# One batch's k and q loads cast to fp16 by their DMA, and the last unit's outputs stored by whole token blocks

## The chip, the cores and the metric

The kernel runs on one core of a Trainium2 chip. The metric is the device time of one execution in microseconds (us). Engines are named as in the profile: PE is TensorE's matrix products and PEld its weight loads, DVE is VectorE, ACT is ScalarE, POOL is GpSimd, SP is SyncE. SP, ACT and POOL also issue DMAs; in a view, SPq, ACTq and POOLq are those issues.

## The reference

Two steps. Linear attention over q, k, v of shape (8 batches, 8 heads, 576 tokens, 64), and a sum of four dense experts over the 4608 tokens of width 512:

```python
q_p, k_p = (phi(q), phi(k))               # phi(x) = (x if x > 0 else exp(x) - 1) + 1
kv = np.einsum('bhsd,bhse->bhde', k_p, v)
z = np.sum(k_p, axis=2)
num = np.einsum('bhsd,bhde->bhse', q_p, kv)
den = np.einsum('bhsd,bhd->bhs', q_p, z)[..., None] + 1e-06
x = num / den                             # then (batch, token, head * 64) as rows of 512
...
p = domain_probs / (domain_probs.sum(-1, keepdims=True) + 1e-09)
for e in range(E):                        # E = 4, w1 512 x 1024, w2 1024 x 512
    h = np.maximum(x @ w1[e], 0.0)
    out += p[:, e:e + 1] * (h @ w2[e])
```

## The kernel before, in words

**Tiles.** A batch's first 512 tokens make one tile of the expert part; the 64 left over of all eight batches make a ninth. So there are nine tiles, `j` = 0 to 8, and with four experts 36 units `(j, e)`. Inside a unit the first product (`Block`, L719 to L782) and the second (`layer2_product`, L643) each use a scheme with seven half-size products in place of eight; GpSimd and VectorE form the sums of operands that it needs (`hidden_sum` L628, `token_sum` L695, `weight_sums` L601, `weight_sums2` L615). Only expert 0 of tile 0, and the second products of tile 0, run in the plain form (`layer1_group` L520, `layer2_part` L574).

**The order of the work.** The program is written out by hand: the lists in `CFG` give each step a position, the steps are sorted by it (L995), and every engine executes its own steps in that order. An instruction that waits holds up everything behind it on its engine. Batch 0's attention comes first (`START`), filled up with warm-up products (L860). Batch `j + 1`'s attention is interleaved with the expert units of tile `j`.

**The loads of the start.** Batch 0 is loaded by SP and ACT. All weights and batch 1's inputs go through GpSimd's queue in the order of `CFG["DMA"]` (`load_first`, L188): first-layer and second-layer weights `w<layer><expert><half>`, cast from fp32 to fp16 by the DMA itself, and batch 1's parts between them: `k0` to `k3`, `q0` to `q3`, `v0` to `v3`, each two heads by 512 tokens, 256 KB in fp32, and `lk`, `lv` for the leftover tokens. In the list's later half: `w110, w111, k0, w120, w121, v0, w210, lk0, w211, lv1, k1, k2, lv0, v1, w131, w130, v2, k3, v3, q1, q0, w220, w221, q2, q3, w230, w231`. The four `v` parts are given fp16 homes (`hs1`, `hs3`), so their DMA casts. Seven of the eight k and q parts have no home of their own: they take fp32 buffers of the pool `praw` (tag `raw`, six buffers, tile name `rawb`). `q2` takes an accumulator's buffer (`acc`, tile name `rawu`). From batch 2 on the inputs are loaded by SP in fp32, into the same `raw` buffers.

**Who reads the parts.** For batch 1, `phi_act` (L303) runs two ScalarE instructions on each k or q part: L310 writes x + 1 as fp16 into `kp` or `qp`, L315 writes exp(x) into PSUM (`psum_ee`). `phi_dve` (L318) then combines the two on VectorE at L322, and does not read the raw part. A v part is copied by ScalarE at L332. `weight_sums` for an expert needs that expert's first-layer weights (L605 is its first instruction).

**The end.** `add_acc` (L562) adds each second product, scaled by the token's probability, to the block's fp32 accumulator (`acc`, 128 tokens x 512 columns). For the last unit, `(8, 3)`, the products come in the order 1, 2, 6, 5, 7, 3, 4, each for the blocks i = 0 and 1 (`layer2_product`, with p the product's number), and alternate between two PSUM banks. Products 1 and 2 end columns 0 to 255 of block i, product 3 ends its columns 256 to 511; product 7 ends columns 256 to 511 of block 2 + i, and product 4 its columns 0 to 255. `store` (L548) writes to the output. A block of tile 8 holds the 64 leftover tokens of two batches, so it takes two DMAs: SP stores the upper half of the partitions, ACT the lower. In the last unit each column half is stored when its last product is added, which makes 16 DMAs of 64 x 256 (64 KB).

Of the kernel before, what the change touches and what calls it, by code (L numbers as in the profile page):

```python
# [10 lines left out]
FP32 = mybir.dt.float32  # L11
FP16 = mybir.dt.float16
# [68 lines left out]
def kernel(  # L81
# [10 lines left out]
    nc = tc.nc  # L92
    ATTN, HSUM, L2ORD, L2AT, MODE = (CFG[x] for x in ("ATTN", "HSUM", "L2ORD", "L2AT", "MODE"))

    B, H, S, D = q.shape
    N, E = moe_domain_probs.shape
    _, Dm, F = moe_w1.shape
# [4 lines left out]
    SM = CM * P  # L102
# [7 lines left out]
    NTILES = N // NT  # L110
# [46 lines left out]
    praw = ctx.enter_context(tc.tile_pool(name="praw", bufs=NRAW))  # L157
# [15 lines left out]
    out_b = out.rearrange("(b s) d -> b s d", s=S)  # L173
# [64 lines left out]
    class Batch:  # L238
# [21 lines left out]
        def load(self, name, i, eng=nc.sync, home=None):  # L260

            src = {"q": q, "k": k, "v": v}[name]
            shape = [P, HQ, CM, D]
            if home is None:
                t = praw.tile(shape, FP32, tag="raw", name="rawb")
            elif home == "h":
                if i % 2 == 0:
                    self.pairs[name] = pm.tile([P, HG, CM, D], FP32, tag="h", bufs=NHB, name="rawh")
                t = self.pairs[name][:, i % 2 * HQ : (i % 2 + 1) * HQ]
            elif home[:2] == "hs":  # L270
                t = pm.tile(shape, FP16, tag=home, bufs=2, name="rawv")
            else:
                t = pm.tile(shape, FP32, tag=home, bufs={"u2": 2, "u3": 1, "acc": NACC}[home], name="rawu")
            h0 = i * HQ
            eng.dma_start(
                out=t, in_=src[self.b, h0 : h0 + HQ, 0:SM].rearrange("h (p c) d -> p h c d", c=CM)
            )
            self.raw[name, i] = t
# [236 lines left out]
    accs = {}  # L515
# [29 lines left out]
    def new_py():  # L545
        return ppm.tile([P, Dm], FP32, tag="py", bufs=2, name="py")

    def store(j, ns, cols=slice(0, Dm)):  # L548
        acc = accs[j, ns][:, cols]
        if j < B:  # L550
            nc.sync.dma_start(
                out=out_b[j, 0:SM].rearrange("(p c) d -> c p d", c=CM)[ns],
                in_=acc,
            )
        else:
            for u in range(2):
                (nc.scalar if u else nc.sync).dma_start(
                    out=out_b[2 * ns + u, SM:S, cols],
                    in_=acc[u * HP : (u + 1) * HP],
                )  # L560

    def add_acc(j, e, ns, ps, ds, first):  # L562
        if (j, ns) not in accs:
            accs[j, ns] = pm.tile([P, Dm], FP32, tag="acc", bufs=NACC, name="acc")
        acc = accs[j, ns][:, ds]
        pscal = p_sb[:, j, ns, e : e + 1]
        if first:
            nc.scalar.activation(acc, ps, AF.Identity, scale=pscal)  # L568
        else:
            nc.vector.scalar_tensor_tensor(  # L570
                out=acc, in0=ps, scalar=pscal, in1=acc, op0=AO.mult, op1=AO.add
            )

    def layer2_part(j, e, ns, hT, part, parts):  # L574
        if part == 0:
            pys[ns] = new_py()
        py = pys[ns]
        for fj in range(part * FC // parts, (part + 1) * FC // parts):
            nc.tensor.matmul(  # L579
                out=py,  # L580
                lhsT=rows(hT, fj)[:, ns * P : (ns + 1) * P],
                rhs=w2_sb[e][:, fj, :],
                start=(fj == 0),
                stop=(fj == FC - 1),
            )
        if part == parts - 1:
            add_acc(j, e, ns, py, slice(0, Dm), e == 0)
            if e == E - 1:
                store(j, ns)
# [53 lines left out]
    def layer2_product(j, e, hT, hss, p, i):  # L643


        if (j, e) == (NTILES - 1, E - 1):
            if p == 1:
                pys[i] = [ppm.tile([P, DH], FP32, tag=tag, bufs=2, name=f"p{tag}") for tag in ("b", "e")]
            run, side = pys[i]
        else:  # L650
            if p == 2:
                pys[i] = new_py()
            run, side = pys[i][:, 0:DH], pys[i][:, DH:Dm]
        ts = slice(i * P, (i + 1) * P)
        ts2 = slice(NH + i * P, NH + (i + 1) * P)
        w, tw = w2_sb[e], t2_sb[e]
        lo, hi = slice(0, FH), slice(FH, FC)
        ps, lhsT, rhs, first = {
            1: (run, lambda k: hT[k // 2][:, k % 2, 0, ts], w[:, lo, 0:DH], (j, e) == (NTILES - 1, E - 1)),
            2: (side, lambda k: hT[k // 2][:, k % 2, 1, ts], w[:, hi, 0:DH], True),  # L660
            5: (side, lambda k: hss[k // 2][0][:, k % 2, ts], tw[:, 0], True),
            6: (run, lambda k: hss[k // 2][1][:, k % 2, ts], tw[:, 1], False),
            7: (run, lambda k: hT[k // 2][:, k % 2, 0, ts2], w[:, lo, DH:Dm], False),
            3: (side, lambda k: hss[k // 2][3][:, k % 2, ts], w[:, hi, DH:Dm], False),
            4: (run, lambda k: hT[k // 2][:, k % 2, 1, ts2], tw[:, 2], False),
        }[p]
        for k in range(FH):
            nc.tensor.matmul(  # L668
                out=ps,
                lhsT=lhsT(k),  # L670
                rhs=rhs[:, k],
                start=first and k == 0,
                stop=k == FH - 1,
                skip_group_check=True,
            )
        c1, c2 = slice(0, DH), slice(DH, Dm)
        ns, ds, first = {
            2: (i, c1, True),
            5: (2 + i, c2, True),
            1: (i, c1, False),  # L680
            6: (i, c2, True),
            7: (2 + i, c2, False),
            3: (i, c2, False),
            4: (2 + i, c1, True),
        }[p]
        add_acc(j, e, ns, ps, ds, first and e == 0)
        if (j, e) == (NTILES - 1, E - 1):
            if p in (2, 3, 4, 7):
                store(j, ns, ds)
        elif e == E - 1 and p in (3, 4):  # L690
            store(j, ns)

    tts = {}

# [107 lines left out]
    def batch_steps(bt, nxt, put, at, at_next):  # L802
# [21 lines left out]
        for m, (n, i) in enumerate(mine):  # L824
            if n == "v":
                put(at[n][i], bt.vcast, i)
            else:
                put(at[n][i], bt.phi_act, n, i)
                put(at[n + "d"][i], bt.phi_dve, n, i)
            if not first:  # L830
                put(at[n][i] + 1, load, m + NRAW)
# [9 lines left out]
        if first:  # L841
            put(at["qtl"], bt.pe_qTl)
            put(at["xl"], bt.pe_xl)
            for i in range(NPAIR):
                put(at["qt"][i], bt.pe_qT, i, nc.scalar)
                put(at["nd"][i], bt.nd_pair, i)
                put(at["xt"][i], bt.pe_xT, i)
            for i in range(NRAW):
                put(at["next"][i], load, len(mine) + i)
        else:  # L850
            put(at["qT"], bt.dma_qT)
            for i in range(6):
                put(at["nd"][i], numerators, 3 * i, min(3, NPAIR * CM - 3 * i))
# [12 lines left out]
    with tc.manual_schedule(  # L866
# [87 lines left out]
        for n, (j, e) in enumerate(units):  # L954
            h, hss = [None, None], [[None] * 4, [None] * 4]
            at = base + 2 * NSLOT * n
            for d in range(2):
                put_block(at + d * NSLOT, j, e, d, h)
            at += 2 * NSLOT + LAG

            def hsum(d, i, hT=h, hss=hss):
                hidden_sum(hT[d], hss[d], i)

            for d in range(2):
                for i in range(4):
                    put_at(at + HSUM[d][i], hsum, d, i)
            order = L2ORD
            if n == len(units) - 1:
                order, at = (1, 2, 6, 5, 7, 3, 4), at + NSLOT
            for m in range(14):  # L970
                put_at(at + L2AT[m], layer2_product, j, e, h, hss, order[m // 2], m % 2)
# [56 lines left out]
```

## Time and profile before

| | us |
|---|---|
| median of 4 runs | 496.43 (495.97 to 496.99) |
| profiled execution, its own time | 496.37 |
| its span (first to last instruction) | 494.5 |
| PE busy in the span | 482.3 |
| last matmul's row begins / last accumulator add ends | 488.55 / 490.11 |
| last store issue begins (SP / ACT) | 491.08 / 491.39 |

Read it so. The span is what the engines' records cover; the execution's own time is 1.87 us longer. The page has busy time by engine, a row of digits over 40 slices of 12.36 us, the chain that ended last (followed back from the last instruction to what released each step), the costliest groups of instructions, and the DMA issues with the time to landing. The trace answers further questions: the waits of one engine in a stretch of time, busy times by stretch, and a list in order of time.

For the loads of the start, these are the landings on GpSimd's queue, each worked out as the start of the issue plus its time to landing (us): w111 30.75, k0 31.4, w120 33.8, w121 36.2, v0 37.0, w210 39.6, lk0 39.7, w211 42.3, lv1 42.5, k1 43.5, k2 44.2, lv0 44.5, v1 44.85, w131 47.3, w130 49.85, v2 50.5, k3 51.2, v3 51.9, q1 52.5, q0 53.25, w220 56.2, w221 60.2, q2 61.2, q3 62.2, w230 64.6. They are read by ScalarE at: k0 31.39, k1 49.69, k2 51.73, k3 53.29, q0 and q1 57.43 and 59.57, q2 61.57, q3 63.56.

### The profile page before, as it was taken

To read this page: it belongs to the slowest core of one execution; us is meant where nothing else is said; L and a number is where in the kernel's file an instruction comes from. 1 tells how busy PE (TensorE), PEld (TensorE's weight loads), DVE (VectorE), ACT (ScalarE), POOL (GpSimd) and SP (SyncE) were. 2 spreads that over 40 slices of the span, in tenths; PEclk is the share of its full clock that TensorE was granted. 3 is DMA by queue.
4 is the path that set the end of the run, shared out by engine and by line. 5 is a ranking of instruction groups with operands and counts; after the bars stand their busy time and mean duration, and the time that the engine had idled before them with its cause. 6 is when DMAs were issued, how large, how long until landed. Compare 5 with 4: busy or idle time off the path is not lost.

```text
span 494.5 us, 11616 instructions
## 1 busy us (share of the span) xinstructions
PE 482.3 (98%) x4346; PEld 409.3 (83%) x4346; DVE 379.1 (77%) x802; ACT 336.4 (68%) x678; POOL 354.5 (72%) x339
## 2 busy tenths in 40 slices
PE   7999989999999999999999999999999999999995
PEld 3556656888898989898989898989898888888884
DVE  5757988798867987698859886888687756775686
ACT  5766969964978488848894789468954565446530
POOL 3735204778967797769776977698669877987774
PEclk9999999999999999999999999999999999999998
DMA  8999976542454245533464245523231020002003
GB/s 257 206 219 238 273 145 177 165 111 52 110 188 116 55 111 162 131 69 93 134 166 80 71 150 139 102 59 91 84 77 32 5 95 1 1 2 86 1 1 87
DMA packets 82201, 53.66 MB, mean 109 GB/s; under 512 B 46240, under 2 KB 75936, under 8 KB 82144
## 3 DMA queue, kind: packets, MB, share of 16 engines
q1 hardware_dynamic: 70592, 40.07, 31.1%
q0 software_dynamic: 9824, 11.27, 12.2%
q10 hardware_dynamic: 1728, 1.57, 1.2%
q8 instruction: 34, 0.56, 0.5%
q14 instruction: 23, 0.19, 0.1%
HBM read 45.16 MB, written 9.44 MB: 110 GB/s over the span
## 4 chain that ended last, share of the span: by engine, by line
PE 83%; DMA 5%; DVE 4%; ACT 4%; POOL 2%; issue 1%; SPq 0%; POOLq 0%; DVEq 0%; ACTq 0%
PE py L668 37%; PE pb L733 23%; PE pe L733 17%; DMA w<-in_moe_w_dram 3%; PE py L579 3%; DVE acc L570 1%; PE psum_nd L465 1%; DMA rawb<-in_v_dram 1%; PE psum_kv L425 1%; DMA out_dram<-acc 1%; ACT u L744 1%; ACT psum_ee L315 1%; POOL w L183 1%; DMA rawh<-in_q_dram 1%; DVE h L717 1%
## 5 line engine op out<-in xcount | busy, mean ns | idle before, releaser
L570 DVE SCALAR_TENSOR_TENSOR acc<-py,p_sb,acc 128x256 f32<-128x256 f32 (+1 forms) x382 | 182.5, 489 | 49.2 <-PE py L668 40.0
L717 DVE CUSTOM_DVE_ANT_0 h<-pe,u 128x512 f16<-128x512 f32 x140 | 96.4, 688 | 41.7 <-PE pe L733 25.4
L733 PEld LDWEIGHTS <-w 128*128 128x128 f16 x1120 | 108.9, 98 | 17.0 <-issue 1.8
L635 POOL TENSOR_TENSOR hs<-h 128x512 f16<-128x512 f16 x64 | 73.9, 1155 | 55.0 <-DVE h L717 53.6
L668 PEld LDWEIGHTS <-h 128*128 128x128 f16 x1024 | 99.6, 98 | 12.2 <-issue 0.9
L668 PE MATMUL py<-w,h 128*128 128x256 f16 x744 | 106.4, 273 | 0.2 <-ACT acc L568 0.2
L744 ACT COPY u<-pb 128x512 f32<-128x512 f32 x140 | 82.8, 592 | 27.5 <-PE pb L733 25.1
L637 POOL TENSOR_TENSOR hs<-hs,h 128x512 f16<-128x512 f16 x64 | 74.7, 1167 | 27.1 <-PE py L668 24.5
L733 PEld LDWEIGHTS <-s 128*128 128x128 f16 x840 | 81.6, 98 | 11.8 <-DVE s L607 0.7
L733 PE MATMUL pb<-tt,w 128*128 128x256 f16 x560 | 84.0, 272 | 0.8 <-ACT u L744 0.7
L668 PEld LDWEIGHTS <-hs 128*128 128x128 f16 x768 | 74.4, 98 | 9.9 <-issue 1.3
L641 POOL TENSOR_TENSOR hs<-h,hs 128x512 f16<-128x512 f16 x64 | 74.5, 1165 | 3.6 <-PE py L668 2.9
L668 PE MATMUL py<-t,hs 128*128 128x256 f16 x496 | 74.4, 272 | 0.6 <-DVE acc L570 0.4
L639 POOL TENSOR_TENSOR h<-h 128x512 f16<-128x512 f16 x64 | 74.5, 1163 | 0.0
L759 ACT ACTIVATE h<-pe 128x512 f16<-128x512 f32 x70 | 41.8, 598 | 44.9 <-PE pe L733 44.4
L753 ACT COPY pe<-pb 128x512 f32<-128x512 f32 x70 | 40.2, 575 | 41.5 <-PE pb L733 14.9
L777 ACT ACTIVATE h<-pb 128x512 f16<-128x512 f32 x70 | 41.9, 599 | 10.4 <-PE pb L733 10.3
L733 PE MATMUL pb<-tt,s 128*128 128x256 f16 x280 | 42.0, 273 | 0.4 <-DVE s L607 0.4
L733 PE MATMUL pe<-tt,s 128*128 128x256 f16 x280 | 42.0, 273 | 0.0
L733 PE MATMUL pb<-xT,w 128*128 128x256 f16 x248 | 37.2, 273 | 0.1
L733 PE MATMUL pe<-xT,s 128*128 128x256 f16 x248 | 37.2, 273 | 0.0
L668 PE MATMUL py<-w,hs 128*128 128x256 f16 x248 | 37.2, 273 | 0.0
(120 smaller groups left out, 604.4 us busy)
## 6 DMA issues: line engine op xcount, KB each, us to landing
out_dram<-acc SPq DMA_DIRECT2D x32, 256.0 KB, 2.5
w<-in_moe_w_dram POOLq DMA_DIRECT2D x14, 512.0 KB, 12.7
rawb<-in_v_dram SPq DMA_DIRECT2D x26, 256.0 KB, 2.8
rawb<-in_q_dram SPq DMA_DIRECT2D x26, 256.0 KB, 2.9
rawb<-in_k_dram SPq DMA_DIRECT2D x26, 256.0 KB, 3.3
w<-in_moe_w_dram POOLq DMA_DIRECT2D x4, 256.0 KB, 6.4
rawb<-in_k_dram POOLq DMA_DIRECT2D x4, 256.0 KB, 10.8
rl<-in_q_dram SPq DMA_DIRECT2D x16, 64.0 KB, 2.6
```

What stands on the lines that cost most here:

```text
L570: nc.vector.scalar_tensor_tensor(out=acc, in0=ps, scalar=pscal, in1=acc, op0=AO.mult, op1=AO.add)
L635: nc.gpsimd.tensor_tensor(out=hs[0], in0=a21, in1=a22, op=AO.add)
L637: nc.gpsimd.tensor_tensor(out=hs[1], in0=hs[0], in1=a11, op=AO.subtract)
L639: nc.gpsimd.tensor_tensor(out=a21, in0=a11, in1=a21, op=AO.subtract)
L641: nc.gpsimd.tensor_tensor(out=hs[3], in0=a12, in1=hs[1], op=AO.subtract)
L668: nc.tensor.matmul(out=ps, lhsT=lhsT(k), rhs=rhs[:, k], start=first and k == 0, stop=k == FH - 1, skip_group_check=True,)
L717: nc.vector._custom_dve(TENSOR_ADD_SAT, out=out, in0=ps, in1=u, s0=BIG, s1=0.0)
L733: nc.tensor.matmul(out=ps[:, kk], lhsT=lk(kc), rhs=rhs[:, kc], start=first and kk == 0 and kc == 0, stop=kc == 1, skip_group_check=True,)
L744: nc.scalar.copy(u, self.b)
L753: nc.scalar.copy(self.e5, self.b)
L759: nc.scalar.activation(self.h[:, :, 0, 0:NH], self.e5, AF.Relu)
L777: nc.scalar.activation(self.h[:, :, 1, 0:NH], self.b, AF.Relu)
```

## The change

Two edits. In `load`, a part without a home is an fp16 tile if it is batch 1's and its name is k or q; the DMA, which GpSimd issues, then casts as it does for v. That holds for k0 to k3, q0, q1 and q3; q2 has the home `acc` and stays fp32, and the leftover parts (`rl`) stay fp32. The buffers of tag `raw` stay six. In `store`, the columns are no longer chosen: the last unit stores a whole block of 128 x 512 after product 3 (blocks 0 and 1) and after product 4 (blocks 2 and 3), again with one DMA by SP and one by ACT, so eight DMAs of 64 x 512 (128 KB). Nothing is stored after products 2 and 7.

Apart from these stores, each engine has the same instructions in the same order with the same waits.

```diff
@@ -262,7 +262,8 @@
             src = {"q": q, "k": k, "v": v}[name]
             shape = [P, HQ, CM, D]
             if home is None:
-                t = praw.tile(shape, FP32, tag="raw", name="rawb")
+                cast = self.b == 1 and name in "kq"
+                t = praw.tile(shape, FP16 if cast else FP32, tag="raw", name="rawb")
             elif home == "h":
                 if i % 2 == 0:
                     self.pairs[name] = pm.tile([P, HG, CM, D], FP32, tag="h", bufs=NHB, name="rawh")
@@ -545,8 +546,8 @@
     def new_py():
         return ppm.tile([P, Dm], FP32, tag="py", bufs=2, name="py")
 
-    def store(j, ns, cols=slice(0, Dm)):
-        acc = accs[j, ns][:, cols]
+    def store(j, ns, last=False):
+        acc = accs[j, ns]
         if j < B:
             nc.sync.dma_start(
                 out=out_b[j, 0:SM].rearrange("(p c) d -> c p d", c=CM)[ns],
@@ -554,8 +555,8 @@
             )
         else:
             for u in range(2):
-                (nc.scalar if u else nc.sync).dma_start(
-                    out=out_b[2 * ns + u, SM:S, cols],
+                (nc.scalar if last and u else nc.sync).dma_start(
+                    out=out_b[2 * ns + u, SM:S],
                     in_=acc[u * HP : (u + 1) * HP],
                 )
 
@@ -684,11 +685,8 @@
             4: (2 + i, c1, True),
         }[p]
         add_acc(j, e, ns, ps, ds, first and e == 0)
-        if (j, e) == (NTILES - 1, E - 1):
-            if p in (2, 3, 4, 7):
-                store(j, ns, ds)
-        elif e == E - 1 and p in (3, 4):
-            store(j, ns)
+        if e == E - 1 and p in (3, 4):
+            store(j, ns, j == NTILES - 1)
 
     tts = {}
 
```

## The prediction

> **What bounds the kernel now.** I read the page's busy shares and chain first, then the chain, the waits and the stretches up to 75 us, where the cast loads lie, and then the last 10 us, where the stores lie.
>
> ```profile
> PE 482.3 (98%) x4346; PEld 409.3 (83%) x4346; DVE 379.1 (77%) x802; ACT 336.4 (68%) x678; POOL 354.5 (72%) x339
> DMA  8999976542454245533464245523231020002003
> ...
> PE 83%; DMA 5%; DVE 4%; ACT 4%; POOL 2%; issue 1%; SPq 0%; POOLq 0%; DVEq 0%; ACTq 0%
> ```
>
> TensorE carries 83% of the chain. The DMA engines are full only in the first six slices (to 74 us), and that is where the seven changed loads are. Neither part of the change touches an instruction of TensorE, so each can only move the start (when the pipeline reaches full speed) or the end (when the last store lands).
>
> Stretches of the start: length, then busy time of PE, PEld, DVE, ACT, POOL, the clock, DMA share and rate:
>
> ```profile
> 30.00:50.00 20.00, 18.92 (x137) 13.13 (x136) 15.43 (x26) 15.07 (x30) 9.87 (x14) 1.00 1.18 228
> 50.00:65.00 15.00, 14.48 (x116) 9.99 (x114) 14.27 (x23) 14.90 (x32) 2.94 (x4) 1.00 1.23 261
> 65.00:75.00 10.00, 8.65 (x74) 5.23 (x72) 8.03 (x23) 5.80 (x13) 1.09 (x2) 1.00 0.46 112
> ```
>
> From 50 to 65 us ScalarE is busy 14.90 of 15 us, and the chain runs through it from 49.17 to 65.24 us with short passages on VectorE. It is bound by ScalarE's own instructions, not by loads. Which waits for loads are left from 28 to 75 us (total, times, longest):
>
> ```profile
> DVE s L605 <- DMA w<-in_moe_w_dram: 9.1, 2, 8.3
> ```
>
> ```profile
> ACT kp L310 <- DMA rawb<-in_k_dram: 0.2, 1, 0.2
> ACT vl L359 <- DMA rl<-in_v_dram: 0.2, 1, 0.2
> ```
>
> So VectorE waits 8.3 us for expert 1's second half (it lands at 30.75 us, ahead of every changed load in the queue) and 0.76 us at 49.92 us for expert 3's. ScalarE waits 0.2 us for k0. That is all that a changed load can lengthen or shorten directly.
>
> The end, in order of time (start, duration):
>
> ```profile
> 488.31 0.92 DVE L570 SCALAR_TENSOR_TENSOR acc<-pe,p_sb,acc 128x256 f32<-128x256 f32 x2
> 489.19 0.92 DVE L570 SCALAR_TENSOR_TENSOR acc<-pb,p_sb,acc 128x256 f32<-128x256 f32 x2
> ...
> 490.74 1.21 ACTq L557 DMA_DIRECT2D out_dram<-acc  x2
> 491.08 0.55 SPq L557 DMA_DIRECT2D out_dram<-acc  x1
> ```
>
> The last add ends at 490.11, but SP's last issue starts at 491.08 and ScalarE's at 491.39 (second of the 490.74 pair). The end is set by store issues in a line, 0.98 and 1.28 us behind the data.
>
> **Part 1, the casts.** Seven loads change: k0 to k3, q0, q1, q3. q2 lives in the accumulators' pool and stays fp32. Nothing is added to or moved on any engine; the instruction order and waits there stay as they are. Each load reads the same 256 KB and writes 128 KB instead of 256 KB.
>
> (a) GpSimd's issue. 0.71 us for the v loads, which are cast already, 0.72 us for k and q: 7 x -0.01 us, and GpSimd has no other work until 73.91 us. Cost 0.
>
> (b) The transfer itself. The rows:
>
> ```profile
> rawb<-in_k_dram POOLq DMA_DIRECT2D x4, 256.0 KB, 10.8
> rawb<-in_q_dram POOLq DMA_DIRECT2D x3, 256.0 KB, 7.7
> rawv<-in_v_dram POOLq DMA_DIRECT2D x4, 128.0 KB, 7.9
> ```
>
> Landing times there are mostly queueing, so I take gaps between successive landings on this queue (issue start plus time to landing). Uncast: k0 0.65 (30.75 to 31.40), k1 1.0, k2 0.67, k3 0.71, q1 0.66, q0 0.71: mean 0.73 us. Cast: v0 0.74, v1 0.35, v2 0.62, v3 0.70: mean 0.60 us. The nearest like pair, k3 and v3 back to back, gives 0.71 and 0.70. Value taken: -0.05 us per load. Lower bound: by written bytes, half of 0.73, -0.36. Upper bound: the trace's packet records show 160 ns for a 4096 B packet of an uncast load and 60 ns for a 512 B packet of a cast one; 64 x 160 against 256 x 60 ns over 16 engines is 0.64 against 0.96 us, +0.32 per load.
>
> [...]
>
> What a shift reaches: expert 3's weights follow three changed loads, so VectorE's 0.76 us wait becomes about 0.6. The chain does not pass through that wait, and VectorE waits 0.7 us for ScalarE at 60.72 us anyway, so I book 0. q2 follows six changed loads: it lands at 61.2 and is read at 61.57 us, 0.36 us of cover. At -0.05 the cover grows; at +0.06 it is gone, and beyond that each load's excess counts six times on ScalarE's chain. k0's own reader waits 0.2 us, but ScalarE idles 0.47 us at 34.6 us, which hides it.
>
> (c) The readers. Fourteen ScalarE instructions (seven at L310, seven at L315) now read fp16. Nearest rows: the copy from cast v takes 626 ns, from fp32 642 (SP's) or 627 ns: 14 x 0 to 16 ns = 0 to -0.22 us. The issue pitch of both kinds is 0.52 us, so I take -0.05 us. VectorE's step (L322) reads kp and PSUM, not the raw tile: 0.
>
> Part 1: -0.05 us, bounds -0.8 to +1.6 (worked out below).
>
> **Part 2, the stores.** Removed: 16 issues of 64x256 (64 KB), eight per queue. Added: eight of 64x512 (128 KB), four per queue, after products 3 and 4. Products 2 and 7 store nothing, so 1.05 MB instead of 0.79 MB must go out after 487.9 us.
>
> Adds of product 3 end at 488.79 and 489.23, of product 4 at 489.67 and 490.11 (0.44 us apart, from the rows above). Issues on SP come 0.645 us apart (488.51, 489.15, 489.79, 490.44, 491.08), so SP issues at 488.82, 489.47, 490.11, 490.76. ScalarE's second issue in both bursts took longer (0.79, 0.85 us), so I put it at 488.82, 489.36, 490.31, 490.96. Last issue: 0.43 us earlier. Two bounds for an issue: 0.36 us (median of the 128x512 stores, L551) and 0.61 us (64-row loads, L253).
>
> To landing:
>
> ```profile
> out_dram<-acc SPq DMA_DIRECT2D x32, 256.0 KB, 2.5
> ...
> out_dram<-acc SPq DMA_DIRECT2D x8, 64.0 KB, 2.0
> ```
>
> Between 2.0 for 64 KB and 2.5 for 256 KB, 128 KB gives 2.2. Before, the stores move at 2 x 64 KB / 0.645 us = 203 GB/s, which is the rate that the trace shows at 490 to 492 us; issue sets it. After, demand doubles to 406 GB/s; the bursts of 256 KB stores reach some 380 GB/s, so 1.05 MB needs 2.76 us from the first byte (488.82 + 1.1 = 489.9) to 492.7, and the last landing comes 0.4 us after the last byte, as before (492.97 to 493.4): 493.1. By issues it is 490.96 + 2.2 = 493.2. Before: 491.39 + 2.0 = 493.4. I take -0.2 us; bounds -0.4 (no late ScalarE issue) and +0.2 (that issue late and 2.6 us to landing).
>
> [...]
>
> **Sum** against the profiled execution's 496.37 us (span 494.5 and 1.87 around it): -0.05 -0.2 = **496.1**. The median of the runs is 496.43, 0.06 above. A difference under 0.2% (1.0 us) is about what measurement cannot tell from no change.
>
> **Rivals.**
> - *Casts slow the queue* (slower). At +0.32 us per load q2 lands 6 x 0.32 = 1.92 us later; less 0.36 us of cover, ScalarE stalls 1.56 us at 61.57 us, where it is the chain: 496.37 + 1.56 - 0.2 = 497.7. It decides from about +0.27 us per load (six loads, less cover and tail gain, over 1.05 us). For it: the packet records. Against: v3's gap equals k3's.
> - *Casts halve the transfer* (faster). At -0.36 expert 3's weights land 1.1 us earlier, the 0.76 us wait goes, and if VectorE passes all of it on: 496.37 - 0.76 - 0.2 = 495.4. Against: v0's gap of 0.74, and the chain passes by that wait.
> - *The tail loses*: the doubled rate is not had, or the early bytes are missed: +0.2, 496.5.
> - *The cast does nothing at all*, as transfer time is set by the read: only the tail counts, 496.2.
>
> **How the numbers follow.** My forecast with the last two rivals, all within 0.2%: 0.80 (forecast 0.45, no effect 0.20, tail 0.15). Slower 0.11: 0.08 for the first rival and 0.03 for a shift of the in-order queues that I have not seen. Faster 0.09: 0.06 for the second rival, 0.03 the same way. The range starts at the faster rival's 495.4 and ends at 496.37 + 0.8 = 497.2, half of part 1's upper bound with a tail that gains nothing; about 0.05 is left out below and 0.1 above.
>
> **What would show it.** Right: k and q rows of 128 KB on GpSimd's queue with landings within 0.5 us of v's; VectorE's wait near 50 us at 0.3 to 0.8 us; no wait of ScalarE for q2; eight 128 KB stores, the last issue near 490.9 in the old time base, landing in 2.1 to 2.4 us. Wrong: a ScalarE wait on rawu or rawb beyond 0.3 us, a TensorE gap from 30 to 75 us that grows or shrinks by over 0.5 us, store landings above 2.6 us, or a moved start of the steady part at 75 us.

## The result, and the profile after

| | before | after |
|---|---|---|
| median, us | 496.57 (53 runs, 495.43 to 497.64) | 497.24 (33 runs, 496.51 to 498.57) |
| profiled execution's own time / its span, us | 496.37 / 494.5 | 496.95 / 495.1 |
| last matmul's row begins, us | 489.31 | 489.01 |
| T, the end of the last accumulator add, us | 490.11 | 489.81 |
| last store's landing, us | 493.41 (T + 3.30) | 493.99 (T + 4.18) |

The ratio of the times is 1.0015, with a 95% interval of 1.001 to 1.002: 0.7 us slower, clear of the scatter, but inside the 0.2% that the forecast called no change. Predicted were 496.1 us (495.4 to 497.2), so the time lies 1.1 us above the forecast and just outside its range. (The last matmul counts by start; before's 488.55 in the table above is the row of a group. Spans, matmuls, T and landings are of the one profiled execution of each kernel.)

The page of after: busy time by engine, the DMA engines' digits, and the chain.

```profile
PE 483.5 (98%) x4346; PEld 409.8 (83%) x4346; DVE 379.0 (77%) x802; ACT 336.4 (68%) x678; POOL 354.5 (72%) x339
DMA  8999975552455235533466246523231020002002
...
PE 84%; DMA 5%; ACT 4%; DVE 3%; POOL 2%; issue 1%; POOLq 0%; DVEq 0%; ACTq 0%
```

Counts and shares are those of before within a point. The two places of the change have to be read by themselves. First the start: stretches (length, busy time of PE, PEld, DVE, ACT, POOL, clock, DMA share, GB/s), the loads on GpSimd's queue (KB, median us to landing), and VectorE's waits for loads from 28 to 75 us (total, times, longest).

```profile
30.00:50.00 20.00, 19.10 (x138) 13.20 (x137) 15.33 (x25) 15.26 (x30) 9.79 (x14) 1.00 1.23 210
50.00:65.00 15.00, 14.53 (x116) 9.94 (x115) 14.31 (x23) 14.90 (x32) 2.91 (x4) 1.00 1.30 233
```

```profile
rawb<-in_k_dram POOLq DMA_DIRECT2D x4, 128.0 KB, 10.9
rawv<-in_v_dram POOLq DMA_DIRECT2D x4, 128.0 KB, 7.7
rawb<-in_q_dram POOLq DMA_DIRECT2D x3, 128.0 KB, 7.2
```

```profile
DVE s L606 <- DMA w<-in_moe_w_dram: 9.3, 3, 8.2
```

The bytes written fall (261 to 233 GB/s from 50 to 65 us), the landings hardly move (before: 10.8 for k, 7.7 for q), and ScalarE's 14.90 us of 15 stay. ScalarE's waits of 0.2 us for `rl` and for k0 are gone; there is none for q2. VectorE's wait near 50 us is 0.90 us (0.76 before), and TensorE's weight loads now wait 0.3 us for one load.

Then the end, in order of time (start, duration, a run of issues as one row):

```profile
488.53 2.48 SPq L558 DMA_DIRECT2D out_dram<-acc  x4
488.53 2.77 ACTq L558 DMA_DIRECT2D out_dram<-acc  x4
488.89 0.92 DVE L571 SCALAR_TENSOR_TENSOR acc<-pb,p_sb,acc 128x256 f32<-128x256 f32 x2
```

T is 488.89 + 0.92 = 489.81. The last issue of SP starts at T + 0.65 and ScalarE's at T + 0.88. What follows those issues is long. The next two blocks show the DMA from 488 to 497 us, in 40 slices of 0.225 us: before, then after (the digits are the DMA engines' busy share; after's issues stand with their median time to landing).

```profile
DMA  0000189699789889789988000000000000000000
GB/s 18 23 9 0 36 196 260 155 209 223 178 200 223 191 187 241 187 196 209 219 187 187 14 0 0 36 0 0 0 0 0 0 0 0 0 0 0 0 0 0
```

```profile
DMA  0000000397999878989899940000000000000000
GB/s 0 0 0 0 0 0 0 73 218 146 246 410 392 301 255 273 346 273 301 246 300 346 355 173 9 0 0 0 0 0 0 0 0 0 0 0 0 0 0 0
...
out_dram<-acc SPq DMA_DIRECT2D x4, 128.0 KB, 2.7
out_dram<-acc ACTq DMA_DIRECT2D x4, 128.0 KB, 3.3
```

Before moves some 200 GB/s from 489.1 us on, steadily. After begins 0.5 us later, touches 410 GB/s for two slices, and falls back to between 246 and 355 (290 in the mean once both queues move bytes), while the engines are mostly 80 to 90% busy. Its eight stores land after 2.4 to 3.5 us, where 2.2 was booked. After's TensorE starts its last matmul 0.3 us earlier; the tail, from the last matmul to the span's end, is 6.08 us in place of 5.19.

### The profile page after: what moved, and what is told of

The parts are those of the page before. It is cut to its first block, busy times and chain, and to the rows that moved or that the text cites. A ratio compares the mean times of both kernels' runs of the same rounds, so it can differ in the third digit from the quotient of the medians.

```text
span 495.1 us, 11600 instructions
## 1 busy us (share of the span) xinstructions
PE 483.5 (98%) x4346; PEld 409.8 (83%) x4346; DVE 379.0 (77%) x802; ACT 336.4 (68%) x678; POOL 354.5 (72%) x339
## 4 chain that ended last, share of the span: by engine, by line
PE 84%; DMA 5%; ACT 4%; DVE 3%; POOL 2%; issue 1%; POOLq 0%; DVEq 0%; ACTq 0%
PE py L669 38%; PE pb L731 23%; PE pe L731 17%; DMA w<-in_moe_w_dram 3%; PE py L580 3%; PE psum_nd L466 1%; DMA rawb<-in_v_dram 1%; DVE acc L571 1%; PE psum_kv L426 1%; DMA rl<-in_k_dram 1%; ACT u L742 1%; POOL w L183 1%; DVE h L715 1%; ACT psum_ee L316 1%; PE pb L669 1%
## 5 line engine op out<-in xcount | busy, mean ns | idle before, releaser
L731 PE MATMUL pe<-xT,w 128*128 128x256 f16 x248 | 37.2, 273 | 0.0
```

The costliest lines, as they stand in the source:

```text
L731: nc.tensor.matmul(out=ps[:, kk], lhsT=lk(kc), rhs=rhs[:, kc], start=first and kk == 0 and kc == 0, stop=kc == 1, skip_group_check=True,)
```

## The experiments

The first theories: the end got longer because bytes were held back (products 2 and 7 store nothing, so 1.05 MB must leave late); or because 128 KB stores are slow where they come late; or because some stage is shared by all stores. The casts were taken to be neutral. All runs but the shared "before" are edits of one **base**: the kernel before with plain copies of as many bytes in place of its DMA transposes. Its output, and that of every run below, is not the reference's; these runs are for their times. T is always the end of the last accumulator add of the run's own profile, of one execution. Each ratio is to executions of before taken beside that run; their medians were 496.28 to 496.56, so a difference of 0.2 to 0.3 us between medians of different rows can be chance.

| run | edit on the base | median, us | ratio to before | last landing |
|---|---|---|---|---|
| base | | 496.29 | 1.0002 (0.9993 to 1.001) | T + 3.38 |
| b_casts | casts | 495.85 | 0.999 (0.9981 to 0.9998) | T + 3.31 |
| b_stores | whole stores | 497.69 | 1.0025 (1.0014 to 1.0035) | T + 4.24 |
| b_late_whole | blocks 0, 1 by quadrants; 2, 3 whole | 496.66 | 1.0005 (0.9996 to 1.0014) | T + 3.35 |
| b_half | blocks 2, 3 whole; 0, 1 not stored | 496.70 | 1.001 (1.0001 to 1.0018) | T + 3.29 |
| b_one_queue | whole stores, all by SP | 499.02 | 1.0055 (1.0043 to 1.0067) | T + 5.52 |
| b_pool7 | product 7's quadrants by GpSimd | 496.39 | 1.0001 (0.9991 to 1.0011) | T + 3.33 |
| b_casts_pool7 | that, and casts | 495.91 | 0.9997 (0.9986 to 1.0009) | T + 3.31 |
| b_both | casts and whole stores | 497.08 | 1.001 (1.0001 to 1.0019) | T + 4.21 |
| b_early_whole | blocks 0, 1 whole; 2, 3 by quadrants | 497.37 | 1.0018 (1.0009 to 1.0027) | T + 3.67 |
| b_rows128_whole | one 128-row store a block | 495.93 | 0.9992 (0.9982 to 1.0002) | T + 2.79 |
| b_rows128_quad | one 128-row store a quadrant | 495.01 | 0.9968 (0.9955 to 0.998) | T + 1.77 |
| b_inter_whole | whole, every second partition | 496.05 | 0.9995 (0.9987 to 1.0004) | T + 3.18 |
| b_inter_quad | quadrants, every second partition | 496.28 | 1.0001 (0.9992 to 1.001) | T + 3.21 |
| b_inter_pool7 | b_pool7, every second partition | 496.19 | 0.9993 (0.9985 to 1.0002) | T + 2.76 |
| b_inter_pool7_casts | that, and casts | 495.93 | 0.999 (0.9982 to 0.9999) | T + 2.77 |

**The base and the two parts.**

```diff
 base: each of four DMA transposes (qT, qTl, xT_left, xT)
-    nc.sync.dma_start_transpose(out=..., in_=...)
+    nc.sync.dma_start(out=..., in_=...)
 b_casts
+    cast = self.b == 1 and name in "kq"
-    t = praw.tile(shape, FP32, tag="raw", name="rawb")
+    t = praw.tile(shape, FP16 if cast else FP32, tag="raw", name="rawb")
 b_stores
-    if p in (2, 3, 4, 7):
-        store(j, ns, ds)
+    if p in (3, 4):
+        store(j, ns)
```

> The base of all experiments: the kernel before, with every DMA transpose (batches 2 to 7 and the leftover tokens of batches 0 and 2 to 7) in place of a transpose a plain copy of as many bytes between the same tiles, so those batches' values are not the reference's. Batch 0's and 1's attention, the loads of the start and the last unit's stores are the same as before. Every theory: within 1 us of the kernel before, as the transposes lie beside a TensorE that is full from 100 to 480 us; TensorE's start times up to 75 us and the tail as in the kernel before (last landing 3.3 us after the last add ends).

> The base with the casts alone; the stores stay by quadrants. Tail theory (all of the changed kernel's +0.7 us is in the last unit's stores): within 0.3 us of the base, last landing 3.3 us after the last add ends. Cast rival (the loads got slower and shifted the start): +0.5 to +0.9 us against the base, all of it in TensorE's start times before 75 us, and the tail unchanged.

> The base with the whole-block stores alone; k and q stay fp32. Tail theory: +0.6 to +0.9 us against the base, the last landing some 4.2 us after the last add ends in place of 3.3. Cast rival: -0.2 us, as the prediction had it for the stores, landing 3.1 us after the last add.

The base has the time of before, and its end. The casts alone are faster by 0.44 us, the whole stores alone slower by 1.40, of which its profile shows 0.86 in the last landing; the other 0.5 is not located. The parts have opposite signs.

**Held bytes, or slow late stores?** Blocks 0 and 1 keep their quadrants, and only blocks 2 and 3 are stored whole; then also without the stores of blocks 0 and 1 at all.

```diff
 b_late_whole                      b_half
-    if p in (2, 3, 4, 7):         -    if p in (2, 3, 4, 7):
-        store(j, ns, ds)          -        store(j, ns, ds)
+    if p in (2, 3):               +    if p == 4:
+        store(j, ns, ds)          +        store(j, ns)
+    elif p == 4:
+        store(j, ns)
```

> The base with blocks 0 and 1 stored by quadrants after products 2 and 3, and blocks 2 and 3 whole after product 4. Leaves 0.79 MB to go after product 3's adds, as little as the kernel before does from product 7 on, but the last two stores of each queue are 128 KB. Theory A (the bytes held back set the end): within 0.3 us of the base, last landing 3.0 to 3.5 us after the last add. Theory B (the size of the last stores sets the end: a 128 KB store of 64 rows lands over 3 us after its issue whatever else is in flight): +0.5 to +0.9 us against the base.

> The base with whole-block stores after product 4 alone; the last unit's blocks 0 and 1 (512 KB of the output) are never stored. Half the bytes, and the same last four 128 KB stores as with whole-block stores. Theory A (bytes held back are what the DMA engines have not yet moved): the last landing 2.8 to 3.1 us after the last add, each store 2.4 to 2.7 us from issue to landing, 0.2 to 0.5 us faster than the base. Rival (a 128 KB store of 64 rows is slow by itself): 3.9 to 4.2 us after the last add and 3.0 to 3.4 us to landing, as when everything is stored whole.

Late stores of 128 KB are not slow by their size alone: in the first run they land 2.4 to 2.5 us after their issue, at T + 3.35. Yet with nothing else in flight, in the second, four of them land after 2.41, 2.73, 2.43 and 3.03 us, T + 3.29, between the two expectations. Its median, 496.70, is 0.4 us above the base's where 0.2 to 0.5 below were expected; its tail, 0.1 us shorter, does not show why. Held bytes are part of the cost of whole stores; something slows these stores even on an empty queue.

**Who issues.** All eight by SP; and product 7's quadrants by GpSimd, which shortens the line of issues of the quadrants (with the casts once more beside it).

```diff
 b_one_queue (with the edit of b_stores)
-    (nc.scalar if u else nc.sync).dma_start(
+    nc.sync.dma_start(
 b_pool7
-    def store(j, ns, cols=slice(0, Dm)):
+    def store(j, ns, cols=slice(0, Dm), pool=False):
...
-    (nc.scalar if u else nc.sync).dma_start(
+    (nc.gpsimd if pool else nc.scalar if u else nc.sync).dma_start(
...
-    store(j, ns, ds)
+    store(j, ns, ds, p == 7)
```

> The base with whole-block stores, all eight issued by SP. Theory C (the two queues share one stage that takes about 0.48 us per 128 KB store, so that the second queue buys nothing): the last landing 4.2 to 4.6 us after the last add, within 0.4 us of whole-block stores on two queues, with an issue every 0.45 to 0.55 us. Rival (each queue's issue costs its own 0.65 us and the queues run beside each other): the last issue 8 x 0.65 us after the first, the last landing 5.9 to 6.3 us after the last add, 2.5 to 3 us slower than the base.

> The base, quadrants, with the four stores after product 7 issued by GpSimd, which has no other work left. Theory A with the issue line (12 late issues on two queues end the base): SP and ACT have four late issues each, the last 0.65 and 0.85 us after the last add in place of 1.03 and 1.37, the last landing 2.7 to 2.9 us after it: 0.4 to 0.6 us faster than the base, if GpSimd's own stores land by then (issue 0.7 us each from product 7's first add: the last lands 2.5 to 3.0 us after the last add). Rival (one shared stage or the DMA engines are full at 200 GB/s with 1 KB rows): within 0.2 us of the base.

> The base with the casts and with product 7's quadrants stored by GpSimd: the candidate that takes the better half of the change and a shorter line of issues. If both gains add: -0.5 us (casts) and -0.4 to -0.6 us (stores), together 0.8 to 1.1 us faster than the base. If the casts' -0.5 us was chance: only the stores' part.

On one queue each store lands 2.33 to 2.37 us after its issue and the landings are 0.64 us apart, so no stage of the stores is shared in the way that theory had it (the last landing, T + 5.52, lies between the 4.2 to 4.6 of the theory and the 5.9 to 6.3 of the rival; the median is 2.7 us above the base's, as the rival had it). I read the 0.64 us at first as the line of issues, which are as far apart. The same window of its DMA says more:

```profile
DMA  0000000000039969979789799799799999200000
GB/s 0 0 0 0 0 0 0 0 0 0 0 73 218 246 164 209 209 191 237 164 210 228 164 246 191 164 255 191 182 228 191 210 209 228 55 0 0 0 0 0
...
out_dram<-acc SPq DMA_DIRECT2D x8, 128.0 KB, 2.4
```

The engines are about 90% busy at some 205 GB/s (128 KB in 0.64 us). So they have little time left to wait for issues; a packet of 2 KB takes 148 ns on average, where a 2 KB packet of the 128-row stores takes 86. The eight stores take the two halves of the partitions in turn, so each half is slow by itself. In b_pool7 the last issues come at T + 0.56 and T + 0.87, near the 0.65 and 0.85 expected, but the landings stretch to 2.5 us, and the end stays at T + 3.33: what the issues gave, the transfers took. With the casts (b_casts_pool7) it is 0.48 us less, the casts' part alone.

**Rows.** The same bytes at the same adds, by DMAs of 128 rows; b_rows128_whole has the edit of b_stores too. They go to 128 neighbouring rows of another place in the output.

```diff
-    for u in range(2):
-        (nc.scalar if u else nc.sync).dma_start(
-            out=out_b[2 * ns + u, SM:S, cols],
-            in_=acc[u * HP : (u + 1) * HP],
-        )
+    turn["st"] = 1 - turn.get("st", 1)
+    (nc.scalar if turn["st"] else nc.sync).dma_start(
+        out=out_b[0, ns * P : (ns + 1) * P, cols], in_=acc
+    )
```

> The base, with each of the last unit's four blocks stored whole by one DMA of 128 rows x 512 (256 KB, SP and ScalarE in turn) to 128 neighbouring rows of batch 0's output in place of the leftover tokens' rows (those are never written, so the output isn't the reference's). As many bytes as the changed kernel's eight 128 KB stores, at the same adds. T is the end of the last accumulator add. Theory (a store of 64 rows moves its bytes slower than one of 128, which is why 1.05 MB took until T+4.2): the stores move at the 380 GB/s of the kernel's other 128-row stores, 2.76 us from a first byte at T-0.2, last landing T+2.5 to T+3.0, and the median 0.3 to 0.9 us under the base's. Rival (late output bytes move at some 290 GB/s here, whatever their rows): 3.6 us from T-0.2 and 0.4 to land, last landing T+3.8 to T+4.2, median 0.5 to 0.9 us over the base's.

> The base, with each column half of the last unit's blocks stored by one DMA of 128 rows x 256 (128 KB, 1 KB rows) to 128 neighbouring rows of batch 0's output (the leftover tokens' rows are never written): the same bytes at the same adds as the base, by half as many DMAs, each of the size of the changed kernel's. Theory (64 rows are slow): no queue is left behind the adds 0.44 us apart, last landing 2.2 to 2.5 us after the last add, median 0.8 to 1.0 us under the base's. Rival (1 KB rows move at some 200 GB/s whatever the number of rows): the 0.79 MB from product 7 on need 3.9 us from T-1.1 and 0.4 to land, last landing T+3.2, median within 0.2 us of the base's.

The theory's numbers came in, in the second run more than in full (T + 1.77 against 2.2 to 2.5). The window of b_rows128_whole, and the issues of b_rows128_quad in it:

```profile
GB/s 0 0 0 0 0 0 27 328 400 382 364 419 355 383 410 364 392 364 391 82 0 0 0 0 0 0 0 0 0 0 0 0 0 0 0 0 0 0 0 0
```

```profile
out_dram<-acc SPq DMA_DIRECT2D x3, 128.0 KB, 1.7
out_dram<-acc ACTq DMA_DIRECT2D x3, 128.0 KB, 1.8
```

The 1.05 MB that the changed kernel moves in 3.80 us from first to last packet go out in 2.89, with most slices near the 380 GB/s that the prediction had booked. A DMA of the changed kernel's size, 128 KB, lands in 1.7 us when it has 128 rows of 1 KB, and its issue takes 0.33 us in place of 0.55. So size, lateness and the length of a row are out, and the number of rows, or where they lie or go, is in.

**Order of the sizes, and the sum of the parts.**

```diff
 b_early_whole
-    if p in (2, 3, 4, 7):
+    if p in (4, 7):
         store(j, ns, ds)
+    elif p == 3:
+        store(j, ns)
```

> The base, with blocks 0 and 1 held back and stored whole after product 3 (four DMAs of 128 KB), and blocks 2 and 3 by quadrants after products 7 and 4, as in the base: the late bytes are the changed kernel's 1.05 MB, but the stores after the last adds are the base's of 64 KB. Theory (a common drain: landings 0.32 us apart for each 64 KB store and 0.44 for each 128 KB store, whoever comes last): the twelve late stores end 8 x 0.32 + 4 x 0.44 less one gap = 4.0 us after a first landing at T-0.2, so at T+3.8, and the median is 0.5 us over the base's. Rival (only the size of the last stores counts): twelve issues in a line as in the base, the last at T+1.3, landed 2.0 later, T+3.3, median as the base's.

> The base with both parts of the change. Theory (the parts do not touch each other: one moves the stretch before 60 us, the other the last 6 us): base's 496.3 + 1.4 of the whole stores - 0.45 of the casts = 497.2 us. Rival (a wait later on takes the casts' gain back once the stores are whole): 497.7 us, as with the whole stores alone.

Small stores behind large ones do not save the end: T + 3.67 against 3.8 expected and 3.3 of the rival; the large ones delay them. And the parts add: 497.08 against 497.2 expected.

**Rows, or half of the partitions?** Number of rows, bytes, issues and queues are left as they are; a pair of stores takes the even and the odd partitions of its block in place of the upper and the lower half, and writes to the same place in the output. b_inter_whole has the edit of b_stores too, b_inter_pool7 that of b_pool7.

```diff
-    in_=acc[u * HP : (u + 1) * HP],
+    in_=acc[u : P : 2],
```

> The base with whole stores, but each pair of 64-row stores takes every second partition of the block (SP the even ones, ScalarE the odd ones) in place of its upper and its lower half; the rows of the leftover tokens' outputs come out permuted. T is the end of the last accumulator add. Theory (half of the 128 partitions is what moves at 203 GB/s by itself): every store now reaches all partitions, runs at some 380 GB/s, and is bounded by its issue: the last issue at T+0.9 as in the changed kernel, 1.7 to 2.2 us to land, last landing T+2.6 to T+3.1, median 1.1 to 1.6 us under the 497.69 of the whole stores by halves. Rival (it is the 64 rows of a DMA that are slow, wherever they lie): last landing T+4.2, median as theirs within 0.3 us.

> The base (quadrants, twelve late stores of 64 KB), each pair taking every second partition of its block instead of the upper and the lower half; rows permuted. Theory (half of the partitions is slow): the landing of a store gets shorter by what half the rate costs on 64 KB, 0.16 us (64 KB at 203 against 390 GB/s), but the line of issues 0.64 us apart on each queue stays, so the last landing only moves from T+3.4 to T+3.2 and the median by 0.1 to 0.3 us. Rival (64 rows are slow wherever they lie): no change, T+3.4, median within 0.1 us of the base's.

> Product 7's four stores issued by GpSimd, as before, which took the line of issues away and gained nothing, and every pair of stores takes every second partition instead of a half; rows permuted. Theory (half of the partitions is slow, and the drain at that rate ate what the shorter line of issues gave): the last issue at T+0.87 lands 1.6 to 2.0 us later, last landing T+2.4 to T+2.9, median 0.5 to 0.9 us under the base's 496.3. Rival (64 rows are slow wherever they lie): T+3.3 as with the halves, median within 0.2 us of 496.4.

> The same with the casts: theory (the casts and the tail add up): 0.45 us under the run beside it, some 495.0 to 495.4 us. Rival (a wait later on takes the casts' gain back): as the run beside it.

The window of b_inter_whole, for comparison with the changed kernel's (same 64-row DMAs, same issue times of 0.55 us):

```profile
DMA  0000000000069999999999960000000000000001
GB/s 0 0 0 0 0 0 0 0 0 0 0 237 401 382 346 401 364 392 364 373 392 373 392 246 0 0 0 0 0 0 0 0 0 0 0 0 0 0 0 36
...
out_dram<-acc SPq DMA_DIRECT2D x4, 128.0 KB, 2.1
out_dram<-acc ACTq DMA_DIRECT2D x4, 128.0 KB, 2.4
```

This settles it. With 64 rows a DMA, but from all over the partitions, the stores run at some 380 GB/s (346 to 401 in the full slices), packets take 86 to 88 ns, the bytes are out in 2.93 us, and the last landing is at T + 3.18 (0.1 beyond the expected range, 1.06 ahead of the halves). The median falls by 1.64 us against b_stores. It is not the number of rows, nor where they go; it is that each store reads one half of the partitions. Against the base, whole stores of this kind land 0.20 us earlier relative to T (3.18 against 3.38) and the median is 0.24 lower: the 0.2 us that the prediction had booked for whole stores. Two smaller readings. In b_inter_quad the packets of 1 KB shorten (75 to 46 ns, medians) and a landing from 2.0 to 1.9 us, but the line of issues stays: T + 3.21 as expected, and of the 0.1 to 0.3 us expected in the median nothing is seen. In b_inter_pool7, where that line is short, the last landing gains 0.57 us (T + 3.33 to 2.76), but the median, 496.19, is only 0.1 us under the base's (0.5 to 0.9 expected) and 0.2 under b_pool7's. Its span ends 1.54 us after the last landing, 1.33 in b_pool7 and 1.10 in the base. Of SP's eight closing semaphore waits, 0.06 us each, four come after the last landing in the base and all eight in these two; the last 0.2 us of b_inter_pool7 is not explained. The casts beside it gave 0.26 us, not 0.45.

## Why the prediction was wrong, point by point

**Part 2, the step that failed.** It is this one: "the bursts of 256 KB stores reach some 380 GB/s, so 1.05 MB needs 2.76 us from the first byte". That rate belongs to stores that read all 128 partitions (b_rows128_whole, 2.89 us). A 64-row store that reads one half of them moves at 205 GB/s when it is alone (b_one_queue). In the changed kernel SP's half goes out alone at 202 GB/s until ScalarE's first packet at T + 0.55; from there on packets of both halves alternate at 290 GB/s in the mean, with 390 to 410 in two slices. Why one half moves at 205 GB/s, and why the two together stay short of 380, is not shown. The mean was 276 GB/s over 3.80 us. With it went the interpolated landing, "128 KB gives 2.2", taken between a row of 64-row and a row of 128-row stores: measured 2.4 to 3.5. In the sum: last landing predicted 0.2 to 0.3 us earlier, found 0.88 later relative to T. Where stores of the same size, number and issue did read all partitions (b_inter_whole), the landing came 0.20 us earlier than the base's, which agrees with the rest of part 2's working.

Before's own trace held the answer, in the packet records that the prediction had open for the loads. A 1 KB packet of the last stores takes 75 ns there (median), which over the 16 DMA engines is 16 x 1024 B / 75 ns = 218 GB/s; a 2 KB packet of the 128-row stores takes 86, which is 381. Of the 203 GB/s of the tail I wrote "issue sets it"; the digits of before, 6 to 9 in that stretch, show the DMA engines nearly full already. Issue and transfer were near the same limit, and lifting one showed the other, as b_pool7 did from the other side.

**The issues** were right to 0.03 us: last ones predicted at T + 0.65 (SP) and T + 0.85 (ScalarE, with its late second issue), found at T + 0.65 and T + 0.88. It is what made the forecast look sound: the issues come 0.4 us earlier, and that is lost behind them.

**The rival "the tail loses"** named the right thing ("the doubled rate is not had, or the early bytes are missed") and priced it at +0.2, since the bound put 2.6 us on the last landing, and not a lower rate on all eight. The measured cost of part 2 is 1.40 us in the medians (b_stores less base), 1.23 (b_both less b_casts), and 0.86 to 0.90 in the last landings of the profiles.

**Part 1, the casts.** Transfer: nearly right. Where three changed loads lie among five, from w130's landing to q0's, the stretch is 3.35 us with casts and 3.46 without, 0.03 a load against 0.05 booked; from w111's landing to q3's it is 31.6 us in after and b_casts, 31.5 in before and 31.9 in the base. Both rivals on the queue fell. Term (c), the readers, was not there: ScalarE's first instruction on a part takes 0.63 us and its second 0.59, in before as in after.

The size is off all the same: -0.05 booked, -0.44, -0.61, -0.48 and -0.26 in the medians of the four pairs on the base, mean -0.45. It lies within the bounds (-0.8 to +1.6). A single pair is hardly clear of its scatter; the four together are. Where the gain lies is seen only in part. TensorE's time from its matmul number 230 to number 330 (about 39 to 54 us) is 15.08 to 15.13 us in five of the 13 profiles without casts and 15.38 to 16.00 in the other eight; with casts it is 15.08 to 15.20 in all five. The same split shows from 230 to 500. But this stretch was picked with the profiles in hand, and with casts the time before matmul 230 and that after matmul 600 are also shorter in the mean, by 0.24 and 0.26 us, against 0.31 us from 230 to 500. So it is a lead, and the place of the gain is not shown.

What is long in the eight: a load near 43 us lands 0.3 to 1.2 us later behind w111 than in before, and ScalarE and the weight loads wait. The waits of the base from 28 to 75 us:

```profile
PEld L579 <- DMA w<-in_moe_w_dram: 0.7, 1, 0.7
ACT vl L359 <- DMA rl<-in_v_dram: 0.6, 1, 0.6
ACT qp L310 <- DMA rawu<-in_q_dram: 0.3, 1, 0.3
```

and of b_casts, where the last two are gone:

```profile
PEld L580 <- DMA w<-in_moe_w_dram: 0.3, 1, 0.3
```

The profiled execution of before was one of the five short ones, with 0.2 us of such a wait; the forecast took one execution's luck for the rule. In after and b_casts a load, lv1, is late by 0.9 us too; there k1 lands 0.27 us behind it, where it takes 0.76 to 0.82 us in the profiles without casts whose lv1 or the load ahead of it was late. That may be how the casts save time. Why loads are late in some executions stays open; no run isolates either, and five profiles are few.

**The sum.** 496.1 forecast; casts 0.4 us better than booked; stores 1.1 to 1.6 us worse; and the medians lie 0.2 us above the profiled execution that the sum started from. That makes 497.0 to 497.5, and 497.24 was measured. That it lies so little outside the range is luck: the casts gave back what the forecast had not booked, and whole stores alone (b_stores) are 1.3 us over the before beside them. **Of the signs named in advance**, landings of k and q like v's and no wait for q2 came in on the side of right, "store landings above 2.6 us" on the side of wrong. VectorE's wait near 50 us was to be 0.3 to 0.8 us, shorter than before's 0.76 by the working, and was 0.90.

**Which version is best.** Casts with the stores by quadrants: 0.999 (0.9981 to 0.9998), measured on the base, ahead of both kernels, but by 0.1% only, within what the forecast called no change. A 128-row store a quadrant is 1.3 us under the base, but a block's rows belong to two batches, 64 each. A layout of the ninth tile that gives one batch every second partition would serve b_inter_pool7's stores; the loads and products for it were not tried.

## What to carry to other kernels

Before booking a rate for a new transfer, take it from rows that read the same partitions, not only the same bytes: the packet's time in the trace, bytes over nanoseconds times the 16 DMA engines, gave 218 GB/s for before's last stores although a line of issues hid it, and stores of one half at a time then moved at 205 (b_one_queue). Fewer and larger stores brought the last issue from T + 1.28 (before) to T + 0.88 (after), and cost where the bytes waited for the last piece: the last landing is at T + 2.79 with one 128-row store a block and at T + 1.77 with one a quadrant. Look at both, and at what the drain can take. And take an average over several executions where a wait of a few tenths of a microsecond decides a term.

## What the runs showed of the hardware

- Stores of 64 partitions in one half, one at a time: 205 GB/s, 148 ns for a 2 KB packet (b_one_queue). With every second partition: some 380 GB/s, 86 to 88 ns (b_inter_whole). Both halves at once from two queues: 290 GB/s in the mean (after).
- Issuing a store of 64 rows took 0.55 us on SP with 64 KB (before) as with 128 KB (after), and 0.56 and 0.61 on ScalarE (medians), 0.64 to 0.66 from one to the next; with every second partition 0.55 too (b_inter_whole). Of 128 rows it took 0.33 to 0.37 us (b_rows128_quad, b_rows128_whole).
- ScalarE's second issue of a burst of 64-row stores took 0.79 to 0.86 us in place of 0.56 in most bursts (before 0.79 and 0.85, after 0.80), and 1.6 to 1.95 in the first burst of six profiles (the base 1.85, where SP's longest took 1.86). Why is open.
- A cast load of 256 KB read and 128 KB written landed nearly as far behind the load ahead of it on GpSimd's queue as an uncast one: 0.65 to 0.69 us for k3, q0, q1 and q3 in after and b_casts, 0.67 to 0.77 for k3, q0 and q1 in before. Single gaps move both ways: k2 behind k1 0.47 to 0.52 us with casts and 0.65 to 0.81 without, v3 behind k3 0.73 to 0.76 with and 0.61 to 0.66 without.
